# Pooled attention and a residual MLP on one core: weight sums laid out by halves, VectorE's order changed in three places, last stores on three queues

## The chip, the core and the metric

The kernel runs on one core of a Trainium2 chip. A core has a matrix engine, TensorE (PE in the profile; its weight loads are PEld), a vector engine (VectorE, DVE), an activation engine (ScalarE, ACT), a general engine (GpSimd, POOL) and a queue engine (SyncE, SP) that mostly issues DMAs. Each engine runs its own list of instructions in order, and waits on semaphores for the others. DMAs are issued by an engine, here SP, ACT or POOL, and are carried out by 16 DMA engines. The metric is the time of one execution in microseconds (us), the median of several runs. Times inside a profile are counted from the start of its span.

## The reference

```python
def _attn_ref(q, k, v):                      # B, H, S, D = 8, 8, 576, 64
    k_p = k.reshape(B, H, Sp, pool, D).mean(axis=3)      # pool = 8, Sp = 72
    v_p = v.reshape(B, H, Sp, pool, D).mean(axis=3)
    scores = scale * np.matmul(q, k_p.transpose(0, 1, 3, 2))
    ...                                      # softmax over the 72 pooled keys
    return np.matmul(attn, v_p)

def _moe_ref(x, alpha1, beta1, w_tok, alpha2, beta2, w_ch1, w_ch2, lam):
    a1 = alpha1 * x + beta1
    tok = np.einsum('ts,bsd->btd', w_tok, a1)
    u = x + lam * tok
    a2 = alpha2 * u + beta2
    ch = np.maximum(a2 @ w_ch1, 0.0) @ w_ch2             # 512 -> 2048 -> 512
    return u + lam * ch
```

The attention's output, with the heads put side by side to 512 columns, is the `x` of the second function. There are 8 x 576 = 4608 rows of 512.

## The kernel before, in words

The 4608 rows are cut into 36 chunks of 128 rows (two batches share a chunk, since 576 is four chunks and a half; the shared one has c = 4), and the chunks into nine blocks of four. Block n does the channel MLP of its four chunks; beside it, in the same stretch of time, the attention and the token mixing of batch n + 1 are computed for later blocks.

Blocks 0 and 1 do the MLP plainly. From block 2 on, the second layer (2048 to 512) is a two by two block product that is done with seven products in place of eight. The products are `L1` to `L7` (function `product`, matmuls on line L1047), and need sums of hidden values (`hidden_sum`, L1016) and sums of weights. VectorE adds the products to the residual in `gather` (steps `g1` to `g7`, L1065; in the last block the single parts of `g3` and `g5`, L1062). In blocks 7 and 8 the first layer (512 to 2048) is done with seven products as well (`hidden_product`, steps `p{q}{i}` with quarter q and product i, L1121). It needs sums of inputs (`sum_inputs`, steps `N0` to `N3`, L1104) and of first-layer weights (`sum_weights`, steps `Sb1` to `Sb4` for the front half of the columns and `Sa1` to `Sa4` for the second, L1094). Each product pair is copied out of or added to by VectorE or ScalarE (`c..`, L1134, and `d..`, L1140), and ScalarE or GpSimd write the hidden values (`r..`, L1150 for GpSimd).

Attention of batch b: SP turns the pooled k by a transposing DMA (`turn_k`, tile `kT`), VectorE finishes the pooling (`pool_k`, L645 and L651, once for each half u of the heads), TensorE computes scores (`att_S4`, L740 and L747), ScalarE the exponential, TensorE the product with v (`att_AV`, L784), and VectorE divides (L791, L793). VectorE also pools v by three additions for each half (`att_V`, L692). Token mixing is L873 on TensorE with the addition of the residual on VectorE (`mix_T`, L880), and the result is transposed by a DMA (`mix_uT`, tile `u_fm`).

Three things set the order. In blocks 0 to 6 each step carries a due time, a number in units of the block's own matmul groups; the steps are sorted by it and issued in that order. Blocks 7 and 8 follow an order written out by hand, the two strings in `late_order`. And waits are made by the tile framework: where two instructions touch overlapping regions of a tile, the later one waits for the earlier. Stores go through `store` (L970 for a plain chunk; L974 for a chunk shared by two batches, which takes two DMAs): in the last block `a0 a1 b0 b1 c0 c1 e0 e1`, where `a` and `e` are halves of the chunks 0 and 1, `b` and `c` halves of the chunks 2 and 3. Chunk 3 of the last block is a shared one.

Behind the last block GpSimd loads a flag, which `good_sums` computed from the softmax sums long before, and branches: if the flag says that the fast softmax, which leaves out the maximum, was out of its safe range, a slow exact version of all the work runs on GpSimd.

```python
again = nc.gpsimd.value_load(flag, min_val=0, max_val=1)    # L1420
with tc.If(again != 0):                                     # L1423
    exact(tc, spare, q, k, v, ...)
```

After that, the program's closing drains and semaphore events are on the last line of the kernel, L1451.

Of the kernel before, what the change touches and what calls it, by code (L numbers as in the profile page):

```python
# [9 lines left out]
BF = mybir.dt.bfloat16  # L10
# [4 lines left out]
P = 128  # L15
SPG = 72
DM = 512
# [193 lines left out]
def kernel(  # L211
# [18 lines left out]
    nc = tc.nc  # L230
# [5 lines left out]
    work = fast.enter_context(tc.tile_pool(name="work", bufs=1))  # L236
# [728 lines left out]
    def store(n, m, c0=0, c1=DM, queues=(nc.sync, nc.sync)):  # L965

        b, c = chunks[4 * n + m]
        u = u_of[n][:, m, c0:c1]
        if c < 4:
            queues[0].dma_start(  # L970
                out=out[b, 0:512, :].rearrange("(p c) d -> p c d", c=4)[:, c, c0:c1], in_=u)
        else:
            for i in range(2):
                queues[i].dma_start(out=out[b + i, 512:576, c0:c1], in_=u[64 * i:64 * i + 64, :])  # L974
# [94 lines left out]
    sums = {}  # L1069
    halves = {"C11": (0, 0), "C12": (0, 1), "C21": (1, 0), "C22": (1, 1)}  # L1070

    def weights_of(i, kc, j):

        if i < 3:
            return w1_of(kc + 2 * (i == 2), j)
        if i == 4:
            return w1_of(kc + 2, j + 8)
        t = sums["W", (1, 2, 3, 4)[(5, 6, 7, 3).index(i)]]
        c0 = 512 * (j // 4)
        return t[:, kc, c0:c0 + 512].rearrange("p (m i) -> p i m", i=4)[:, j % 4, :]  # L1080

    def sum_weights(i, g):

        if ("W", 1) not in sums:
            for k in range(2):
                t = work.tile([P, 2, 2, 1024], BF, tag="v_u", bufs=2, name="w1_s")
                sums["W", 1 + 2 * k], sums["W", 2 + 2 * k] = t[:, 0], t[:, 1]
        cols = slice(512 * g, 512 * g + 512)
        W = {k: sums["W", k][:, :, cols] for k in range(1, 5)}
        lo, hi = w1[0][:, :, cols], w1[1 + g]  # L1090
        a, b, op = {1: (hi[:, 0:2], hi[:, 2:4], ALU.add), 2: (W[1], lo[:, 0:2], ALU.subtract),
                    3: (lo[:, 0:2], hi[:, 0:2], ALU.subtract),
                    4: (lo[:, 2:4], W[2], ALU.subtract)}[i]
        nc.vector.tensor_tensor(out=W[i], in0=a, in1=b, op=op)  # L1094

# [59 lines left out]
    def block_plan(n, other):  # L1155

        plan = {"gd": good_sums}
        for q in range(4):
            for i in range(1, 8):
                plan[f"p{q}{i}"] = lambda q=q, i=i: hidden_product(n, q, i)  # L1160
            for i in range(1, 4):
                c = f"c{q}{i}"
                plan[c] = lambda q=q, i=i, c=c: hidden_copy(n, q, i, c in other)
                plan[f"d{q}{i}"] = lambda q=q, i=i: hidden_add(n, q, i)
            for k, key in (("X", "C11"), ("B", "C12"), ("Y", "C21"), ("Z", "C22")):
                for a in range(2):
                    r = f"r{q}{k}{a}"
                    plan[r] = lambda q=q, key=key, a=a, r=r: hidden_out(n, q, key, a, r in other)
        for k in range(2):
            for a in range(2):  # L1170
                t = mlp_A(n, 6 + 8 * k + a)
                plan[f"h3{'lh'[k]}{a}"] = plan[f"r3{'lh'[k]}{a}"] = lambda t=t: next(t, None)
        for g in range(2):
            for i in range(1, 5):
                plan[f"S{'ba'[g]}{i}"] = lambda i=i, g=g: sum_weights(i, g)
                plan[f"s{i}{g}"] = lambda i=i, g=g: hidden_sum(n, i, g)
        for i in range(1, 8):
            for pp in range(2):
                plan[f"L{i}{pp}"] = lambda i=i, pp=pp: product(n, i, pp)
                plan[f"g{i}{pp}"] = lambda i=i, pp=pp: gather(n, i, pps=(pp,))  # L1180
            plan[f"g{i}"] = lambda i=i: gather(n, i)
        for part in range(2):
            plan["g7" + "ab"[part]] = lambda part=part: gather(n, 7, part)
        for i in range(4):
            plan[f"N{i}"] = lambda i=i: sum_inputs(n + 1, 1 + i)
            plan[f"w{i}"] = lambda m=i: store(n, m)
        for m in range(2):
            both = (nc.sync, nc.scalar)
            plan[f"a{m}"] = lambda m=m: store(n, m, 0, HALF)
            plan[f"b{m}"] = lambda m=m: store(n, 2 + m, HALF, DM, both)  # L1190
            plan[f"c{m}"] = lambda m=m: store(n, 2 + m, 0, HALF, both)
            plan[f"e{m}"] = lambda m=m: store(n, m, HALF, DM, (both[m],) * 2)
        return plan

# [61 lines left out]
    def attention(b):  # L1256


        first = b == 1
        todo = []  # L1260
        if first:
            for hp in range(4):
                todo.append((2.6 + 0.9 * hp, lambda hp=hp: whole(att_F(b, hp))))
            todo.append((3.5, lambda: cast_rem(b, nc.gpsimd, behind=nc.vector)))
            for u in range(2):
                todo.append((3.65 + 0.1 * u, lambda u=u: load_w2(2 + u)))
            todo.append((7.4, lambda: whole(att_Frem(b, nc.scalar.copy))))
        if b < B - 1:
            at = 28.5 if first else 10.0
            todo.append((at, lambda: whole(att_F(b + 1, 0))))  # L1270
            todo.append((at + 0.1, lambda: whole(att_F(b + 1, 2))))
            todo.append((19.3 if first else 23.1, lambda: cast_rem(
                b + 1, nc.gpsimd, behind=None if first else nc.vector)))
            todo.append((26.72 if b > 1 else 27.2, lambda: whole(att_Frem(b + 1))))
        for u in range(2):
            if first:
                todo.append((3.6 + 0.1 * u, lambda u=u: sum_k(b, u, nc.gpsimd)))
            if 1 < b < B - 1:
                todo.append((26.5 + 0.1 * u, lambda u=u: sum_k(b + 1, u, nc.gpsimd)))
                todo.append((26.73 + 0.1 * u, lambda u=u: turn_k(b + 1, u)))  # L1280
            if b > 2:
                todo.append((4.1 + 2.0 * u, lambda u=u: pool_k(b, u)))
                continue
            if first:
                todo.append((19.1 + 0.1 * u, lambda u=u: sum_k(2, u, nc.gpsimd)))
            todo.append((7.0 + 2.3 * u if first else 2.9 + 2.0 * u,
                         lambda u=u: whole(
                             att_K(b, u, nc.vector.tensor_copy if first else nc.scalar.copy))))
        for u in range(2):
            at = (9.0 if first else 6.3, 13.6)[u]  # L1290
            todo.append((at, lambda u=u: att_S4(b, u)))
            for k, dt in enumerate((0.1, 0.1, 0.1, 0.7, 1.7, 1.75) if u else (0.1, 0.1, 0.1, 1.1, 2.1, 3.1)):
                todo.append((at + dt, lambda u=u, k=k: st1[b]["exp", u](k)))
            early = (5.2, 5.7, 3.7, 4.2) if first else (5.7, 6.2, 2.9, 3.4)
            for i, dt in enumerate((2.9, 3.4, 4.6, 5.1) if u else early):
                h = 4 * u + i
                todo.append((at + dt, lambda h=h: whole(att_AV(b, h))))
                if i % 2:
                    eng = nc.gpsimd if h == 5 or first and h < 5 else nc.vector
                    todo.append((at + dt + 0.1, lambda h=h, eng=eng: att_X(b, h - 1, h + 1, eng)))  # L1300
        for u in range(2):
            when = (0.2, 1.4, 2.2), (10.0, 12.8, 13.0) if b == 2 else (5.0, 7.2, 8.0)
            if first:
                when = (10.6, 10.7, 10.8), (12.5, 12.6, 12.7)
            for i, at in enumerate(when[u]):
                todo.append((at, lambda u=u, i=i: att_V(b, u, 4 >> i)))
        for c in range(5):
            at = 22.0 + 1.1 * c if first else 21.0 + (1.3 if b == 2 else 1.15) * c
            if c < 4 or b % 2:
                todo.append((at, lambda c=c: whole(mix_T(b, c))))  # L1310
                key = (b, c) if c < 4 else (b - 1, 4)
                todo.append((at + 1.8, lambda key=key: whole(mix_uT(key))))
        return todo
# [11 lines left out]
        SUMS + 1: (  # L1325
# [10 lines left out]
    for n in range(NBLK):  # L1336
# [54 lines left out]
                todo.append((27.2 if m < 2 else 29.2, lambda m=m: store(n, m)))  # L1391
        if n == SUMS - 1:
            for i in range(1, 5):
                todo.append((27.3 + 0.01 * i, lambda i=i: sum_inputs(n + 1, i)))
        if n == 0:
            todo.append((6.2, lambda: whole(setup_rowsum(4))))
            todo.append((10.0, lambda: load_lam(nc.vector)))
# [58 lines left out]
```

## Time and profile before

| | |
|---|---|
| median of 3 runs | 328.36 us (328.30 to 328.98) |
| the profiled execution | 328.99 us, span 327.5 us |
| TensorE busy | 318.5 us, 97% of the span, 2556 matmuls |
| VectorE busy | 259.5 us, 79% |
| ScalarE busy | 180.3 us, 55% |
| GpSimd busy | 133.1 us, 41% |

A row of a timeline gives the start and the length in us, the engine and line, the operation with the tile written and the tiles read, and in brackets the idle time of the engine ahead of it with the instruction that ended it; rows with xN hold N instructions in a row. The lengths of TensorE's matmuls are modelled and overlap, so that the step from one start to the next is what counts. Rows of an engine's name with a q (POOLq, SPq) belong to its instruction queue: loads of registers, branches, events, drains and DMA issues, which are not counted as busy.

### The profile page before, as it was taken

To read this page: it belongs to the slowest core of one execution; us is meant where nothing else is said; L and a number is where in the kernel's file an instruction comes from. 1 tells how busy PE (TensorE), PEld (TensorE's weight loads), DVE (VectorE), ACT (ScalarE), POOL (GpSimd) and SP (SyncE) were. 2 spreads that over 40 slices of the span, in tenths; PEclk is the share of its full clock that TensorE was granted. 3 is DMA by queue.
4 is the path that set the end of the run, shared out by engine and by line. 5 is a ranking of instruction groups with operands and counts; after the bars stand their busy time and mean duration, and the time that the engine had idled before them with its cause. 6 is when DMAs were issued, how large, how long until landed. Compare 5 with 4: busy or idle time off the path is not lost.

```text
span 327.5 us, 6744 instructions
## 1 busy us (share of the span) xinstructions
PE 318.5 (97%) x2556; PEld 214.8 (66%) x2556; DVE 259.5 (79%) x538; ACT 180.3 (55%) x353; POOL 133.1 (41%) x155
## 2 busy tenths in 40 slices
PE   8899999999999999999999999999999999999994
PEld 3689654455444576657675676567755766988983
DVE  6783578987599979786967796878697889888984
ACT  3868999278224843396139612881278136823920
POOL 8587467994274022601180018002600650711900
PEclk9999999999999999999999999999999999999999
DMA  7999999868997971698549944997470034003003
GB/s 198 203 230 255 213 175 284 141 191 158 193 214 117 219 211 35 102 280 154 155 76 268 172 137 87 164 222 204 90 163 0 2 65 146 0 2 109 23 20 112
DMA packets 73352, 47.43 MB, mean 145 GB/s; under 512 B 41282, under 2 KB 64098, under 8 KB 73318
## 3 DMA queue, kind: packets, MB, share of 16 engines
q1 hardware_dynamic: 59302, 34.78, 45.2%
q0 software_dynamic: 12896, 11.28, 22.3%
q10 hardware_dynamic: 1120, 0.92, 0.9%
q8 instruction: 20, 0.33, 0.4%
q14 instruction: 14, 0.11, 0.1%
HBM read 38.31 MB, written 9.44 MB: 146 GB/s over the span
## 4 chain that ended last, share of the span: by engine, by line
PE 81%; DVE 5%; DMA 5%; POOL 3%; issue 3%; ACT 2%; POOLq 0%; SPq 0%; DVEq 0%; ACTq 0%
PE ps_h L930 27%; PE ps_w L1047 23%; PE ps_tok L873 11%; PE ps_ch L951 8%; PE ps_m L1121 5%; DMA v<-in_v_dram 2%; DMA kT<-k_bf 2%; PE ps_av L784 2%; PE ps_s L740 2%; POOL k_bf L362 1%; ACT H L938 1%; DVE x_tm L793 1%; POOL k_raw L360 1%; DVE u_sb L1065 1%; DVE w_s L1094 1%
## 5 line engine op out<-in xcount | busy, mean ns | idle before, releaser
L930 PE MATMUL ps_h<-u_fm,w 128*128 128x512 bf16 (+2 forms) x496 | 108.8, 366 | 0.6 <-ACT u_fm L905 0.4
L938 ACT ACTIVATE H<-ps_h,bias_cols 128x512 bf16<-128x512 f32 x116 | 79.0, 688 | 37.7 <-PE ps_h L930 36.4
L930 PEld LDWEIGHTS <-w 128*128 128x128 bf16 x496 | 53.0, 114 | 39.6 <-issue 2.1
L1047 PEld LDWEIGHTS <-H 128*128 128x128 bf16 x560 | 53.4, 98 | 10.4 <-DVE u_sb L1065 1.2
L884 ACT CAST u_bf<-u_sb 128x512 bf16<-128x512 f32 x34 | 21.0, 618 | 70.0 <-issue 41.5
L807 POOL TENSOR_TENSOR xs<-x_tm,lamal_bc 128x512 bf16<-128x512 f32 x12 | 15.2, 1270 | 103.8 <-DVE x_tm L793 103.5
L1047 PE MATMUL ps_w<-w,H 128*128 128x256 bf16 x448 | 53.6, 273 | 0.0
L1065 DVE TENSOR_TENSOR u_sb<-u_sb,ps_w 128x512 f32<-128x512 f32 x54 | 36.1, 684 | 12.0 <-PE ps_w L1047 11.5
L873 PE MATMUL ps_tok<-xs,wtT 128*128 128x512 bf16 (+5 forms) x220 | 45.1, 361 | 0.0
L793 DVE TENSOR_TENSOR x_tm<-ps_av,recs 128x320 f32<-128x320 f32 x64 | 31.5, 492 | 2.7
L880 DVE TENSOR_TENSOR u_sb<-x_tm,ps_tok 128x512 f32<-128x512 f32 (+1 forms) x40 | 27.2, 683 | 7.5 <-PE ps_tok L873 7.3
L769 ACT ACTIVATE ET<-ps_s 72x512 f16<-72x512 f32 x56 | 32.3, 590 | 0.0
L951 PE MATMUL ps_ch<-w,H 128*128 128x512 bf16 x128 | 30.4, 379 | 0.0
L873 PEld LDWEIGHTS <-wtT 128*128 128x128 bf16 (+3 forms) x220 | 19.2, 100 | 15.2 <-issue 1.1
L791 DVE RECIPROCAL recs<-ps_av 128x5 f32<-128x5 f32 x64 | 12.1, 188 | 17.4 <-PE ps_av L788 17.1
L692 DVE TENSOR_TENSOR v_u<-v_u 72x1024 f32<-72x1024 f32 (+1 forms) x24 | 23.9, 995 | 0.2
L1047 PE MATMUL ps_w<-w_t,h_s 128*128 128x256 bf16 x168 | 22.6, 272 | 0.0
L951 PEld LDWEIGHTS <-H 128*128 128x128 bf16 x128 | 12.0, 98 | 13.9 <-issue 0.4
L360 POOL TENSOR_TENSOR k_raw<-k_raw 128x512 f32<-128x512 f32 x14 | 19.1, 1366 | 2.2 <-DMA k_raw<-in_k_dram 2.2
L362 POOL TENSOR_TENSOR k_bf<-k_raw 128x512 bf16<-128x512 f32 x14 | 19.1, 1364 | 1.1
L1047 PEld LDWEIGHTS <-h_s 128*128 128x128 bf16 x168 | 16.4, 98 | 4.2
L784 PEld LDWEIGHTS <-ET 72*128 72x128 f16 x256 | 13.8, 97 | 5.6 <-ACT ET L726 0.2
(188 smaller groups left out, 470.6 us busy)
## 6 DMA issues: line engine op xcount, KB each, us to landing
out_dram<-u_sb SPq DMA_DIRECT2D x29, 256.0 KB, 3.9
k_raw<-in_k_dram SPq DMA_DIRECT2D x13, 512.0 KB, 4.4
v_u<-in_v_dram SPq DMA_DIRECT2D x12, 512.0 KB, 6.1
q_bf<-in_q_dram POOLq DMA_DIRECT2D x15, 256.0 KB, 5.1
w<-in_moe_w_ch_dram POOLq DMA_DIRECT2D x6, 512.0 KB, 13.2
out_dram<-u_sb SPq DMA_DIRECT2D x11, 128.0 KB, 2.8
v<-in_v_dram POOLq DMA_DIRECT2D x4, 288.0 KB, 10.6
w<-in_moe_w_ch_dram POOLq DMA_DIRECT2D x1, 1024.0 KB, 14.0
```

Of the source, the lines that this page charges most:

```text
L360: eng.tensor_tensor(out=raw[:, :, 0:2], in0=raw[:, :, 0:2], in1=raw[:, :, 2:4], op=ALU.add)
L362: eng.tensor_tensor(out=bf, in0=twice[0], in1=twice[1], op=ALU.add)
L692: nc.vector.tensor_tensor(out=out, in0=source[:, :, 0:width], in1=source[:, :, width:2 * width], op=ALU.add)
L769: nc.scalar.activation(out=o, in_=i, func=AF.Exp, bias=0.0, scale=0.125 if b < 3 else 0.125 * 0.125)
L793: nc.vector.tensor_tensor(out=x[:, 1 - odd:6 - odd, dd:dd + D], in0=av[:, :, 0:64], in1=rec.unsqueeze(2).to_broadcast((P, 5, D)), op=ALU.mult)
L873: nc.tensor.matmul(out=ps_tok[p0:p1, cols], lhsT=wtT[0:kk, at, P * c:P * c + p1 - p0], rhs=xs_pool[i][0:kk, sc, cols], start=(sc == 0), st ...
L880: nc.vector.tensor_tensor(out=s["u"][p0:p1, :], in0=x[p0:p1, 1 + c if c < 4 else 5 - 5 * i, :], in1=ps_tok[p0:p1, 0:DM], op=ALU.add)
L930: nc.tensor.matmul(out=ps_h[:, t0:t1 + one], lhsT=w1_of(cc, j), rhs=rhs, start=(cc == 0), stop=(cc == 3))
L938: nc.scalar.activation(out=H4[n, j // 4][:, j % 4, :], in_=ps_h, func=AF.Relu, bias=bias_cols[:, j:j + 1], scale=1.0)
L951: nc.tensor.matmul(out=ps, lhsT=H_of(n, j)[:, 128 * m:128 * m + 128], rhs=w2[j // 4][:, j % 4, :], start=(j == 0), stop=(j == NJ - 1))
L1047: nc.tensor.matmul(out=ps, lhsT=stat(j), rhs=moving(j), stop=(j == 7), start=(first and (pp == 0 or alone) and j == 0), skip_group_check=True)
L1065: nc.vector.tensor_tensor(out=o, in0=o, in1=banks[key, "both"], op=ALU.add)
```

## The change

Five edits, each of which leaves the arithmetic as it is:

1. The four sums of first-layer weights, each 128 x 2 x 1024 before with the two halves as column ranges, are laid out as two contiguous blocks of 128 x 1024, one for each half.
2. In block 6 the input sums for block 7 have earlier due times: 25.3 and 25.31 for the first two, 26.0 and 26.01 for the others, where all four had 27.3.
3. In block 7 the gather `g3` and the stores of chunks 0 and 1 stand ahead of the last product's second half (`L71`) and of its gathers and stores.
4. The second half's `pool_k` has due time 8.95 in place of 6.1, which puts it behind two value sums and two hidden sums on VectorE in five blocks.
5. The stores `b` and `c` of the last block are spread over SP, ACT and POOL. Before, SP issued b0, b1's first part, c0, c1's first part and e0, and ACT issued b1's and c1's second parts and e1. After, SP issues b0, c1's second part and e0, ACT issues b1's and c1's first parts and e1, and POOL issues b1's second part and c0, both ahead of the flag's load. `b1`'s parts wait for gather `g7b`, and `c0` for gather `g4`.

TensorE's and ScalarE's order of instructions is the same in both kernels.

```diff
 def weights_of(i, kc, j):
-        c0 = 512 * (j // 4)
-        return t[:, kc, c0:c0 + 512].rearrange("p (m i) -> p i m", i=4)[:, j % 4, :]
+        return t[:, j // 4, kc, :].rearrange("p (m i) -> p i m", i=4)[:, j % 4, :]
 def sum_weights(i, g):
-                t = work.tile([P, 2, 2, 1024], BF, tag="v_u", bufs=2, name="w1_s")
+                t = work.tile([P, 2, 2, 2, 512], BF, tag="v_u", bufs=2, name="w1_s")
-        W = {k: sums["W", k][:, :, cols] for k in range(1, 5)}
+        W = {k: sums["W", k][:, g] for k in range(1, 5)}
 def block_plan(n, other):
-            both = (nc.sync, nc.scalar)
+            both, third = (nc.sync, nc.scalar), nc.gpsimd
+            q_b, q_c = ((nc.sync,), (nc.scalar, third))[m], ((third,), (nc.scalar, nc.sync))[m]
-            plan[f"b{m}"] = lambda m=m: store(n, 2 + m, HALF, DM, both)
-            plan[f"c{m}"] = lambda m=m: store(n, 2 + m, 0, HALF, both)
+            plan[f"b{m}"] = lambda m=m, to=q_b: store(n, 2 + m, HALF, DM, to)
+            plan[f"c{m}"] = lambda m=m, to=q_c: store(n, 2 + m, 0, HALF, to)
 def attention(b):
-                todo.append((4.1 + 2.0 * u, lambda u=u: pool_k(b, u)))
+                todo.append(((4.1, 8.95)[u], lambda u=u: pool_k(b, u)))
 late_order, block 7:
-            "... N0 N2 N1 L30 N3 L31 L70 L71 g7a g7b w2 w3 g3 w0 w1",
+            "... N0 N2 N1 L30 N3 L31 L70 g3 w0 w1 L71 g7a g7b w2 w3",
 block 6:
-                todo.append((27.3 + 0.01 * i, lambda i=i: sum_inputs(n + 1, i)))
+                todo.append(((25.3, 25.31, 26.0, 26.01)[i - 1], lambda i=i: sum_inputs(n + 1, i)))
```

2 rows, old and new, of the table late_order are left out of this document.

## The prediction

> **What bounds the kernel now.** I read the page first, for the busy shares and the chain, then PE's waits in the late blocks, then timelines around each wait, and last the issue rows after the last matmul. All times are us from the start of the span.
>
> ```profile
> span 327.5 us, 6744 instructions
> PE 318.5 (97%) x2556; PEld 214.8 (66%) x2556; DVE 259.5 (79%) x538; ACT 180.3 (55%) x353; POOL 133.1 (41%) x155
> PE 81%; DVE 5%; DMA 5%; POOL 3%; issue 3%; ACT 2%; POOLq 0%; SPq 0%; DVEq 0%; ACTq 0%
> ```
>
> TensorE (PE) carries 81% of the chain and is busy 97% of the span. The change adds and removes no matmul, so it can win only where PE waits and after PE's last matmul. From 268 on, PE's waits are these two groups:
>
> ```profile
> PE ps_m L1121 <- DVE w_s L1094: 1.0, 2, 0.7
> PE ps_m L1121 <- DVE h_q L1134: 0.4, 1, 0.4
> ```
>
> The profiled execution took 328.99, 1.49 more than its span and 0.63 more than the median of the runs, 328.36.
>
> **Part 1: weight sums half by half (L1072 to L1094).** Before, the two halves of a sum are column ranges of one tile, interleaved in memory. PE around the waits:
>
> ```profile
> 276.24 0.27 PE L1121 MATMUL ps_m<-u_s,w_s 128*128 128x256 bf16 x1
> 276.75 0.52 PE L1121 MATMUL ps_m<-u_s,w_s 128*128 128x256 bf16 x3 [0.24 <-DVE w_s L1094]
> 277.11 0.60 PE L1121 MATMUL ps_m<-u_fm,w 128*128 128x256 bf16 x4
> 277.54 0.27 PE L1121 MATMUL ps_m<-u_s,w_s 128*128 128x256 bf16 x1
> 278.55 0.52 PE L1121 MATMUL ps_m<-u_s,w_s 128*128 128x256 bf16 x3 [0.74 <-DVE w_s L1094]
> ```
>
> and VectorE (DVE) beside them:
>
> ```profile
> 274.99 0.68 DVE L1094 TENSOR_TENSOR w_s<-w,w 128x1024 bf16<-128x1024 bf16 x1
> 276.00 0.69 DVE L1094 TENSOR_TENSOR w_s<-w_s,w 128x1024 bf16<-128x1024 bf16 x1 [0.33 <-PE ps_m L1121]
> ...
> 277.81 0.69 DVE L1094 TENSOR_TENSOR w_s<-w,w 128x1024 bf16<-128x1024 bf16 x1
> ```
>
> By the written order of block 7 (front half Sb, second half Sa) the held products are p06 and p17, which read half 0 of sums 2 and 3. Half 0 of sum 3 is the row at 274.99, done at 275.67, and sum 2 stands before it. But the waits end with the other half: Sa2 at 276.00 + 0.69 = 276.69 and Sa3 at 277.81 + 0.69 = 278.50. PE is held for sums that it does not read, and Sa2 itself waited 0.33 for PE in the same way. Four unbroken matmuls take 277.54 − 277.11 = 0.43, or 0.11 each. So the stretch 276.24 to 276.75 lost 0.51 − 0.11 = 0.40, and 277.54 to 278.55 lost 1.01 − 0.11 = 0.90. With each half contiguous those dependences are gone, and the sums that PE does read were done at least 0.6 before it asks. **−1.3.** What would be late next are ACT and POOL (55% and 41% busy), which write the hidden values after PE; I take nothing from them. The sums keep size and type, so 0.69 should hold.
>
> **Part 2: input sums earlier, in block 6.** Four L1104 instructions of 0.42 move ahead on DVE, the first two past the last token-mix addition, which starts after an idle 0.52:
>
> ```profile
> 268.07 1.38 DVE L880 TENSOR_TENSOR u_sb<-x_tm,ps_tok 64x512 f32<-64x512 f32 x2 [0.52 <-PE ps_tok L873]
> ...
> 270.52 0.42 DVE L1104 TENSOR_TENSOR u_s<-u_fm 128x512 bf16<-128x512 bf16 x1
> ```
>
> PE has no wait on any of them. Two take 2 × 0.42 = 0.84, less the idle 0.52: at most +0.3 for the last chunk's transpose, whose reader has other products ahead of it; and the weight sums behind may start up to 0.3 earlier, which after part 1 nobody waits for. **0**, ends −0.3 and +0.3.
>
> **Part 3: g3 and stores w0, w1 ahead of the last product, block 7.** PE, then DVE:
>
> ```profile
> 297.74 2.35 PE L1121 MATMUL ps_m<-u_fm,w 128*128 128x256 bf16 x20
> 300.48 1.03 PE L1121 MATMUL ps_m<-u_s,w_s 128*128 128x256 bf16 x8 [0.39 <-DVE h_q L1134]
> ```
> ```profile
> 297.94 1.88 DVE L1065 TENSOR_TENSOR u_sb<-u_sb,ps_w 128x512 f32<-128x512 f32 x3 [0.69 <-PE ps_w L1047]
> 299.75 0.68 DVE L1134 COPY h_q<-ps_m 128x512 f32<-128x512 f32 x1
> ```
>
> At 297.94 DVE starts three gathers together, because g7a and g7b wait for the last product and g3 stands behind them; the copy for which PE waits starts at 299.75. With g3 ahead, one of three (1.88 / 3 = 0.63) moves into the 0.69 that DVE idles, so the copy starts about 0.6 earlier and PE's wait ends. Twenty matmuls at 0.11 last issue at 297.74 + 19 × 0.11 = 299.83, the next would be at 299.94: the loss is 300.48 − 299.94 = **−0.53**. SP issues w0 and w1 earlier and w2, w3 later, with nothing behind them for 20 us.
>
> **Part 4: second pooled-k addition later, in five blocks.**
>
> ```profile
>   DMA kT<-k_bf: 4.0, 3
> ```
> ```profile
> 176.78 0.42 DVE L645 TENSOR_TENSOR kp<-kT 128x256 bf16<-128x256 bf16 x1 [2.02 <-DMA kT<-k_bf]
> 178.98 0.69 DVE L1016 TENSOR_TENSOR h_s<-H 128x1024 bf16<-128x1024 bf16 x1
> ```
> ```profile
> 182.76 0.30 PE L740 MATMUL ps_s<-qT,kp 64*72 64x256 bf16 x1 [0.20 <-DVE x_tm L793]
> ...
> 182.97 0.28 PE L740 MATMUL ps_s<-qT,kp 64*72 64x256 bf16 x1
> 183.38 1.49 PE L930 MATMUL ps_h<-u_fm,w 128*128 128x512 bf16 x6
> ```
>
> Three of these additions (L645) hold DVE 4.0 in all for a transposing DMA; of the blocks concerned PE feels it in this one. There two value sums and two hidden sums now go first. They end at 178.98 + 0.69 = 179.67 today, up to 2.02 earlier without the wait, so the addition ends between 178.1 and 180.1, and the scores that read it, which PE works on at 182.76, keep over 2 us. PE's loss there is at most 0.20 shown plus the hole 182.97 to 183.38 less a step of 0.11, 0.3, so **0 to −0.5**. Whether the DMA is that late in the median run isn't known. It could be what separates 328.99 from 328.36; then it is worth −0.5 against the profiled run, and 0 against the median.
>
> **Part 5: last stores on three queues.** The same eight DMAs; SP loses b1's first part and c0, ACT swaps its two parts for two others, POOL takes b1's second part and c0. Today, SP's first and last issue of five, ACT's last, the landing view of these stores, and DVE's last additions:
>
> ```profile
> 321.96 0.33 SPq L970 DMA_DIRECT2D out_dram<-u_sb  x1
> ...
> 324.06 0.54 SPq L970 DMA_DIRECT2D out_dram<-u_sb  x1
> ```
> ```profile
> 323.72 0.37 ACTq L970 DMA_DIRECT2D out_dram<-u_sb  x1
> ```
> ```profile
> DMA to landing us min/median/max: 2.5/2.5/2.5
> ```
> ```profile
> 320.64 1.88 DVE L1065 TENSOR_TENSOR u_sb<-u_sb,ps_w 128x512 f32<-128x512 f32 x3 [0.46 <-PE ps_w L1047]
> 322.44 0.41 DVE L1062 TENSOR_TENSOR u_sb<-u_sb,ps_w 128x256 f32<-128x256 f32 x1
> 323.26 0.42 DVE L1062 TENSOR_TENSOR u_sb<-u_sb,ps_w 128x256 f32<-128x256 f32 x1 [0.40 <-PE ps_w L1047]
> ```
>
> The last landing is 324.06 + 2.5 = 326.56. With SP relieved, e0 goes out near 323.1, after its addition (322.44 + 0.41 = 322.85), and the last to land is e1, issued by ACT at 323.72 as now: 326.2. For the transfers alone: −0.35, at best −0.9 (e0's whole advance).
>
> ```profile
> 323.00:324.50 1.50, 0.23 (x3) 0.00 (x0) 0.42 (x1) 0.00 (x0) 0.00 (x0) 1.00 0.88 237
> ```
>
> The DMA engines are 88% busy just after the last matmul, so more queues share them. The Trainium skill, page "DMA: Bandwidth & Descriptors", section "Issuing engines are not separate DMA queues", says that transfers issued by different engines run on the same 16 engines and that only the issuing time is saved; by that the gain is the 0.35 and not the 0.9.
>
> **What POOL has behind its stores.** POOL ends the program: it loads a flag and branches over the slow version of the kernel. Rows by line:
>
> ```profile
> L1420 POOLq TENSOR_LOAD <-flag x1: 502/502/502, 310.3 to 310.3; - x1
> ```
> ```profile
> L1423 POOLq EVENT_SEMAPHORE  x2: 17/17/17, 313.8 to 313.9; - x2
> L1423 POOLq COMPARE_BRANCH  x1: 50/50/50, 311.2 to 311.2; - x1
> ```
> ```profile
> L1451 POOLq EVENT_SEMAPHORE  x4: 17/17/17, 326.7 to 327.4; - x4
> L1451 POOLq DRAIN  x3: 46/102/2770, 314.0 to 327.2; - x3
> ```
>
> Load at 310.3; branch at 311.2; then nothing until 313.8 (2.6 gone behind a taken branch); then a drain at 314.0. The 2.77 drain must be this first one, as the others stand at the closing events from 326.7 on. So the path takes 314.0 + 2.77 − 310.3 = 6.5 and ends at 316.8, hidden today, since the stores keep everyone until 326.7. That cover goes. After the change POOL's queue holds b1's second part and c0 first, and c0 waits for g4, the end of DVE's three gathers, 320.64 + 1.88 = 322.5. How long POOL takes to issue one is seen early in the kernel:
>
> ```profile
> L371 POOL DMA_DIRECT2D wt_bf<-in_moe_w_tok_dram x2: 573/581/589, 6.5 to 7.1; - x2
> ```
>
> So the load starts between 322.5 (no issue time) and 323.1 (0.58), and POOL is ready for the closing events between 329.0 and 329.6, or 329.9 if the branch's fetch runs 0.3 longer among the stores. Against 326.7 that is +2.3 to +3.2; I take c0's issue as shown, 323.1, and +2.8, since fetch and drain have a row each. The landing gain vanishes under it. The Trainium skill, page "Runtime: NRT & Kernel Launch", section "Instruction fetch mechanics", speaks against this edit too: a taken branch to outside the loaded window waits for a DMA fetch of the target. The 2.6 row agrees.
>
> **Sum.** Profiled run: 328.99 − 1.3 − 0.53 − 0.5 + 2.8 = 329.5. From the median: 328.36 − 1.3 − 0.53 + 2.8 = 329.3 if the late DMA was not in it, 328.8 if it was. I take **329.2**, the likeliest case's own range being 328.5 to 330.0.
>
> **The rivals.** Differences under 0.2%, 0.66, count as none: 327.7 to 329.0.
>
> Other side, faster: the drain is short. The other two POOL drains took 0.05 and 0.10, and what the 2.77 does isn't shown; if it belongs to the moment (a fetch that the stalled queue has since done), the path is 6.5 − 2.7 = 3.8, ready at 326.3 to 326.9, −0.4 to +0.2 against now, and the time is 328.36 − 1.83 − 0.4 … + 0.2 = 326.1 to 326.7. It turns at a path of 6.5 − (2.8 − 1.83) = 5.5: a drain under 1.8 makes the kernel faster. Against it: the one execution shown has the row, and the branch target is the same. The Trainium skill, page "VectorE: DVE Perf Modes", section "The DRAIN you can't avoid", gives closing drains as about 12 ns on all engines; by it the time is as in this case, but the 2770 ns row disagrees.
>
> Slower still: parts 1 and 3 give nothing, because the wait only changes its name (DVE at 79% hands PE the next sum late, or POOL's hidden values come late): 328.36 + 2.8 = 331.2, or 330.2 with half the gain. For it: DVE is busy 79% of the span, and more than that among those sums. Against: the half that the held products read was done 0.6 and more before.
>
> Doing nothing: the late DMA of part 4 does not recur and part 2 is hidden; that is inside the main case's range.
>
> **How the numbers follow.** Path pays in full 0.61: three quarters of it above 329.0, the rest within 0.2%. Short drain 0.26, all faster. Gains lost 0.13, nearly all slower. Faster 0.27, same 0.17, slower 0.56. The range, 326.2 to 330.2, holds the short drain, the main case and the nearer end of the lost gains, because the drain has ends on both sides.
>
> **What would show it.** Right: no L1121 wait on L1094 or on L1134 at g3; POOL's load after 321 instead of 310, a gap of 2.6 behind its branch, a drain of 2.8, and closing events some 2 behind the last landing. Wrong: a short drain, closing events straight after the landing, or new PE waits in the last two blocks.

## The result and the profile after

The changed kernel takes 330.53 us (median of 5 runs, 330.12 to 330.71); the kernel before took 328.37 beside it. It is slower by a ratio of 1.006, 95% interval 1.0045 to 1.0075. The forecast said 329.2, with 326.2 to 330.2 as its range: the direction was right, the size too small, +0.8 where +2.2 came, and the time lies above the range.

PE did win what it was to win. This is the view of all its waits over the whole span of the changed kernel (us in all, times, longest):

```profile
PE ps_warm L862 <- DVE early L402: 1.5, 1, 1.5
PE ps_v L680 <- DMA v<-in_v_dram: 0.4, 1, 0.4
PE ps_sc L702 <- ACT kp L671: 0.4, 1, 0.4
PE ps_h L930 <- ACT u_fm L905: 0.4, 1, 0.4
PE ps_bc L496 <- DVE part L476: 0.2, 1, 0.2
PE ps_w L516 <- DMA wt_bf<-in_moe_w_tok_dram: 0.2, 1, 0.2
```

No L1121 wait is left (the line is L1120 now); the rest are from the start of the kernel. The tail undoes it. First DVE's last additions in the changed kernel's timeline, then POOL's rows by line. In the latter the counts are followed by the shortest, median and longest duration in ns and by the first and the last start.

```profile
318.42 1.88 DVE L1065 TENSOR_TENSOR u_sb<-u_sb,ps_w 128x512 f32<-128x512 f32 x3 [0.47 <-PE ps_w L1047]
320.22 0.41 DVE L1062 TENSOR_TENSOR u_sb<-u_sb,ps_w 128x256 f32<-128x256 f32 x1
321.04 0.42 DVE L1062 TENSOR_TENSOR u_sb<-u_sb,ps_w 128x256 f32<-128x256 f32 x1 [0.41 <-PE ps_w L1047]
```
```profile
320.00 0.58 POOL L974 DMA_DIRECT2D out_dram<-u_sb  x1 [10.71 <-DVE u_sb L1065]
320.60 0.58 POOL L970 DMA_DIRECT2D out_dram<-u_sb  x1
```
```profile
L1420 POOLq TENSOR_LOAD <-flag x1: 688/688/688, 320.6 to 320.6; - x1
```
```profile
L1423 POOLq EVENT_SEMAPHORE  x2: 17/17/17, 325.1 to 325.2; - x2
L1423 POOLq COMPARE_BRANCH  x1: 45/45/45, 321.6 to 321.6; - x1
```
```profile
L1451 SPq EVENT_SEMAPHORE  x12: 17/28/1109, 321.5 to 328.9; - x12
L1451 POOLq EVENT_SEMAPHORE  x4: 17/17/17, 328.2 to 328.9; - x4
L1451 POOLq DRAIN  x3: 46/103/2933, 325.2 to 328.7; - x3
L1451 SPq DRAIN  x3: 7/7/13, 325.4 to 328.4; - x3
```

DVE ends its last addition at 321.46 (321.04 + 0.42); before, that was at 323.68, so the computing ends 2.2 earlier. POOL's closing events begin at 328.2, 6.7 later; before, it was 326.7 − 323.68 = 3.0. The tail grew by 3.7. POOL loads the flag at 320.6, branches at 321.6, goes on at 325.1 and drains for 2.93. SP waits for the landings and for POOL's event at 325.1, and has its first drain at 325.4, so every store has landed 2.8 or more before POOL's closing events.

Some executions of the later comparisons ran at a lower granted clock (0.97 to 0.98) and took at least 3.6 us longer; the medians and ranges below leave them out, the ratios of the late flag and of the earlier input sums still hold some of them, and the late flag's profile is one of them.

### The profile page after: what moved, and what is told of

The parts are those of the page before. It is cut to its first block, busy times and chain, and to the rows that moved or that the text cites. A ratio compares the mean times of both kernels' runs of the same rounds, so it can differ in the third digit from the quotient of the medians.

```text
span 329.0 us, 6714 instructions
## 1 busy us (share of the span) xinstructions
PE 316.2 (96%) x2528; PEld 214.8 (65%) x2556; DVE 259.4 (79%) x538; ACT 179.9 (55%) x353; POOL 134.6 (41%) x157
## 4 chain that ended last, share of the span: by engine, by line
PE 89%; DMA 3%; POOL 2%; ACT 2%; DVE 1%; issue 1%; POOLq 0%; DVEq 0%; ACTq 0%
PE ps_h L930 30%; PE ps_w L1047 26%; PE ps_tok L873 12%; PE ps_ch L951 8%; PE ps_m L1120 6%; DMA wt_bf<-in_moe_w_tok_dram 3%; PE ps_s L740 2%; PE ps_av L784 2%; ACT H L938 1%; PE ps_r L747 1%; POOL v L308 1%; PE ps_av L788 1%; ACT ET L769 0%; DVE h_xs L1133 0%; ACT u_fm L905 0%
## 5 line engine op out<-in xcount | busy, mean ns | idle before, releaser
L930 PE MATMUL ps_h<-u_fm,w 128*128 128x512 bf16 (+2 forms) x478 | 107.2, 366 | 1.2 <-ACT u_fm L905 0.4
```

The costliest lines, as they stand in the source:

```text
L930: nc.tensor.matmul(out=ps_h[:, t0:t1 + one], lhsT=w1_of(cc, j), rhs=rhs, start=(cc == 0), stop=(cc == 3))
```

## The experiments

**The changed kernel with the old stores.** Edits 1 to 4 stay, edit 5 goes.

```diff
-            both, third = (nc.sync, nc.scalar), nc.gpsimd
-            q_b, q_c = ((nc.sync,), (nc.scalar, third))[m], ((third,), (nc.scalar, nc.sync))[m]
+            both = (nc.sync, nc.scalar)
...
-            plan[f"b{m}"] = lambda m=m, to=q_b: store(n, 2 + m, HALF, DM, to)
-            plan[f"c{m}"] = lambda m=m, to=q_c: store(n, 2 + m, 0, HALF, to)
+            plan[f"b{m}"] = lambda m=m: store(n, 2 + m, HALF, DM, both)
+            plan[f"c{m}"] = lambda m=m: store(n, 2 + m, 0, HALF, both)
```

> The changed kernel with its last stores on SP and ACT alone, as before. Theory 1 (POOL's end path, from the flag's load to the closing drain, ends last because stores stand ahead of it): the path is hidden again, PE's gains stay: 328.4 - 1.3 - 0.5 = 326.5, or 326.0 if the late kT transfer also counts. Theory 2 (the moved sums and additions cost time somewhere, and the tail only shows it): 328.4 or more.

Measured: 326.42 (326.25 to 326.54) beside 328.50 of the kernel before, ratio 0.9934, 0.9921 to 0.9947. POOL's rows of the closing line are those of before again:

```profile
L1450 POOLq EVENT_SEMAPHORE  x4: 17/17/17, 324.3 to 324.9; - x4
L1450 POOLq DRAIN  x3: 46/103/2770, 311.5 to 324.8; - x3
L1450 SPq DRAIN  x3: 7/7/13, 324.2 to 324.5; - x3
```

The long drain starts at 311.5 and is over ten us before the closing events (311.5 + 2.77 = 314.3, against 324.3), and the closing events follow SP's first drain, 324.2. So the loss is in edit 5 alone; edits 1 to 4 are worth 2.1.

**The kernel before with three queues.** Edit 5 alone, as in the diff of the change.

> The kernel before with the last stores on three queues and nothing else. Theory 1: the tail grows by what the profile after shows, from 3.5 to 7.15 between the end of the last matmul and POOL's closing events, +3.6: 332.0. The forecast's own sizes (2.6 behind the branch, 2.8 of drain) give +2.8: 331.2. Theory 2: about 328.4, the tail costing nothing by itself.

Measured: 332.16 (331.90 to 332.43; ratio 1.0109, 1.0093 to 1.0125), 3.7 above the 328.50 of the kernel before beside it. By itself the edit costs as much as the profile after says. Taking it away from the changed kernel gained 4.1. The profiles lie between: 3.7 in the tail, and some 0.2 outside the span, since the changed kernel's profiled execution took 1.71 more than its span (330.71 − 329.0), against 1.49 before and 1.54 with the old stores. That makes 3.9; the 0.2 to either side are not accounted for.

**The flag's load ahead of the stores.** The branch stays behind them.

```diff
+                if n > SUMS and name == "b0":
+                    again = nc.gpsimd.value_load(flag, min_val=0, max_val=1)
                 todo[name]()
...
-    again = nc.gpsimd.value_load(flag, min_val=0, max_val=1)
```

> The changed kernel with POOL's load of the flag ahead of its two stores, the branch still behind them. If the path is a plain chain (load, branch, fetch, drain), the load's 1.0 drops out: 329.5. If the fetch behind the branch waits until the stores' transfers are through (it started when they ended), an earlier branch only waits longer: 330.3 to 330.5.

Measured: 329.16 (328.79 to 329.46), 1.4 below the changed kernel: more than the plain chain's 1.0, and the rival's 330.3 is out. POOL's rows at the branch and the close:

```profile
L1424 POOLq EVENT_SEMAPHORE  x2: 17/17/17, 323.8 to 323.9; - x2
L1424 POOLq COMPARE_BRANCH  x1: 50/50/50, 320.5 to 320.5; - x1
```
```profile
L1452 POOLq EVENT_SEMAPHORE  x4: 17/17/17, 327.0 to 327.6; - x4
L1452 POOLq DRAIN  x3: 46/103/2933, 324.0 to 327.5; - x3
```

The branch is 1.1 earlier (320.5, not 321.6), goes on 3.3 later, and the same drain follows; the closing events are 1.2 earlier (327.0, not 328.2). What stands ahead of the branch moves the end about one for one.

**A near target for the branch.** The slow version is replaced by one memset.

```diff
     with tc.If(again != 0):
-        exact(tc, spare, q, k, v, ...)
+        nc.gpsimd.memset(spare.tile([1, 8], FP, name="spare"), 0.0)
```

> The changed kernel with the slow version behind the branch replaced by one memset, so that the branch's target is near (the fallback for unsafe softmax sums is left out). If gap and drain are code fetches behind a far jump: the gap of 3.45 and the drain of 2.9 go, POOL is ready before the last store lands, and the time is 326.0, as low as without POOL's stores or 0.3 lower. If they belong to the branch or to POOL's drain behind its own DMAs: 330.5, with the drain still at 2.8 or more.

Measured: 326.74 (326.66 to 327.24), ratio 0.9945, 0.9932 to 0.9958: 0.3 above the old stores, where 0 to 0.3 below was expected. The rows at the branch and the close:

```profile
L1423 POOLq COMPARE_BRANCH  x1: 54/54/54, 321.5 to 321.5; - x1
L1423 POOLq EVENT_SEMAPHORE  x1: 17/17/17, 321.7 to 321.7; - x1
```
```profile
L1450 POOLq EVENT_SEMAPHORE  x4: 17/17/17, 324.8 to 325.4; - x4
L1450 POOLq DRAIN  x3: 46/101/2933, 321.8 to 325.2; - x3
L1450 SPq DRAIN  x3: 7/7/13, 324.2 to 325.0; - x3
```

This parts the two terms, which the expectation had taken together. The gap behind the branch falls from about 3.4 (3.5 by starts that are rounded to 0.1, 3.4 by the sum of the path further down) to 0.2: it belonged to the far target. The Trainium skill, page "Runtime: NRT & Kernel Launch", section "Instruction fetch mechanics", says that a taken branch to outside the loaded window has to wait until a DMA has fetched the target, and this pair of rows agrees. The drain stays at 2.93, with no far target and no fetch beside it, so it is not a code fetch; what it does is open. POOL's closing events, at 324.8, still come 0.6 behind SP's first drain, so with this drain behind its stores POOL is the last to end even here. The same rows price edit 5's transfers. SP's first drain, after its last landing, is at 324.2 here with three queues and at 324.2 with two. DVE's last addition ended at 321.33 (320.91 + 0.42) here and at 321.24 (320.82 + 0.42) there, so three queues landed the stores 0.1 sooner, not 0.35:

```profile
320.91 0.42 DVE L1062 TENSOR_TENSOR u_sb<-u_sb,ps_w 128x256 f32<-128x256 f32 x1 [0.41 <-PE ps_w L1047]
```
```profile
320.82 0.42 DVE L1062 TENSOR_TENSOR u_sb<-u_sb,ps_w 128x256 f32<-128x256 f32 x1 [0.40 <-PE ps_w L1047]
```

**A late flag without stores on POOL.** The old stores, and POOL copies one element of chunk 2 behind `c0` ahead of the flag's load.

```diff
... (the stores as in the first experiment; spot is a new tile of one element)
                 todo[name]()
+                if n > SUMS and name == "c0":
+                    nc.gpsimd.tensor_copy(out=spot, in_=u_of[n][0:1, 2, 0:1])
```

> The changed kernel with its last stores on SP and ACT alone, and on POOL one copy of a single element of chunk 2 behind gather g4, ahead of the flag's load: POOL's end path starts as late as with the stores, but POOL issues no DMA. If the longer path (the fetch came 1.8 behind the branch where it was 0.94, the drain took 2.93 where it was 2.77) is owed to the stores' traffic on the DMA engines: the same lengths, 330.3 to 330.5. If it is owed to POOL's own two DMA issues: 0.94 and 2.77 again, 329.2 to 329.5.

Measured: 329.82 (329.54 to 330.30), 1.6 above the 328.19 of the kernel before beside it (ratio 1.0022, 0.998 to 1.006), between the two expectations. The rows split the question. POOL's rows at the branch and the close, of which only the steps from one to the next are read:

```profile
L1425 POOLq EVENT_SEMAPHORE  x2: 17/17/17, 329.9 to 330.0; - x2
L1425 POOLq COMPARE_BRANCH  x1: 50/50/50, 326.6 to 326.6; - x1
```
```profile
L1453 POOLq DRAIN  x3: 46/103/2770, 330.1 to 333.4; - x3
```

The long drain is 2.77 again: its extra 0.16 goes with POOL's own DMAs. The gap stays long, 3.3. To see why, the DMA view of a window shows the instruction queue, q14, and the stores' queues (packets, MB, share of the 16 engines). The kernel before, 312.1 to 312.7:

```profile
q14 instruction: 1, 0.01, 4.4%
```

the changed kernel, first 321.6 to 323.4 and then 323.4 to 323.9:

```profile
q10 hardware_dynamic: 185, 0.17, 37.6%
q1 hardware_dynamic: 212, 0.18, 35.1%
q0 software_dynamic: 49, 0.13, 21.0%
```
```profile
q14 instruction: 1, 0.01, 3.9%
```

and the late flag, 328.2 to 328.7:

```profile
q10 hardware_dynamic: 96, 0.09, 50.7%
q1 hardware_dynamic: 72, 0.06, 43.4%
q14 instruction: 1, 0.01, 3.8%
```

Before, the fetch's packet came 0.9 to 1.5 after the branch (311.2), on idle DMA engines. In the changed kernel nothing of q14 moves until 1.8 after the branch, while the stores hold 94% of the engines; with the late flag it is 1.6 or more, with no store on POOL. From the start of the packet's window to POOL's next row it is 1.7 in all three (312.1 to 313.8, 323.4 to 325.1, 328.2 to 329.9), so the longer gap is all ahead of the packet. So the fetch is held up by the stores' transfers, whoever issues them, though not until they are all through: in the last window it moves among them. How they hold it up is not shown.

**The other edits one by one, on the kernel before.** Each is the edit's own part of the change's diff.

> The kernel before with the weight sums laid out half by half and nothing else. Theory 1 (the waits were for the other half's sum): both L1094 waits gone, 328.4 - 1.3 = 327.1. Rival (the waits only take another name): 328.4, with a new PE wait in the same place.

Measured for the weight sums by halves: 327.01 (326.80 to 327.43), ratio 0.9956, 0.9938 to 0.9973: −1.3 against 328.32. PE's waits from 268 on in that kernel:

```profile
PE ps_m L1120 <- DVE h_q L1133: 0.4, 1, 0.4
```

Both waits for the sums are gone and none took their place; the rival falls.

> The kernel before with g3 and its stores ahead of L71 and nothing else. Theory 1: the wait for the copy of h_q gone, 328.4 - 0.5 = 327.9. Rival (the gathers g7a and g7b, now later, hold the next products): 328.4 or more.

Measured for g3 ahead of L71: 327.76 (327.57 to 328.66), ratio 0.998, 0.9967 to 0.9994: −0.6. From 268 on PE waits only for the weight sums:

```profile
PE ps_m L1121 <- DVE w_s L1094: 1.0, 2, 0.7
```

> The kernel before with the second pooled-k addition later and nothing else. If the kT transfer is late in every execution: 328.4 - 0.5 = 327.9 and its spread falls. If it is late only in the executions near 329.0: about 328.3, the high ones gone. Theory 2 (the addition now comes late for the scores): above 328.4 with a PE wait of L740 or L747 on kp.

Measured for the later pooled-k addition: 328.28 (328.08 to 328.60) beside 328.32 (327.90 to 329.80), ratio 0.9998, 0.9987 to 1.0009. The median does not move. Five of the 23 runs of the kernel before stood above 328.6, none of these nine; chance alone would do that about once in nine times, so the runs don't show that the high ones are gone. The traces say what a high execution is. Here are DVE's first and second pooled-k addition in the block of part 4 and the first of the next block, in the kernel before (profiled at 328.99; its second one is in the prediction, with a wait of 2.02), then in the weight sums by halves (327.43, the highest of its runs), then in the kernel before with three queues:

```profile
172.01 0.41 DVE L645 TENSOR_TENSOR kp<-kT 128x256 bf16<-128x256 bf16 x1
...
207.32 0.41 DVE L645 TENSOR_TENSOR kp<-kT 128x256 bf16<-128x256 bf16 x1
```
```profile
172.17 0.41 DVE L645 TENSOR_TENSOR kp<-kT 128x256 bf16<-128x256 bf16 x1
...
176.68 0.42 DVE L645 TENSOR_TENSOR kp<-kT 128x256 bf16<-128x256 bf16 x1 [1.77 <-DMA kT<-k_bf]
...
207.23 0.42 DVE L645 TENSOR_TENSOR kp<-kT 128x256 bf16<-128x256 bf16 x1
```
```profile
171.98 0.41 DVE L645 TENSOR_TENSOR kp<-kT 128x256 bf16<-128x256 bf16 x1
...
175.12 0.42 DVE L645 TENSOR_TENSOR kp<-kT 128x256 bf16<-128x256 bf16 x1 [0.39 <-DMA kT<-k_bf]
...
206.56 0.41 DVE L645 TENSOR_TENSOR kp<-kT 128x256 bf16<-128x256 bf16 x1
```

From the first row to the last it is 35.31, 35.06 and 34.58: 0.7 and 0.5 more where DVE waited 2.02 and 1.77 for the kT transfer than where it waited 0.39, which is about what these two executions stand above their medians (0.6 and 0.4). PE's list of waits shows 0.20 of it in the one and nothing in the other, so that list alone would have missed it.

> The kernel before with block 6's input sums earlier and nothing else. Theory 1: 328.4, hidden. Bounds of the forecast: -0.3 to +0.3.

Measured for the earlier input sums: 328.11 over five runs, beside 328.19 over fifteen of the kernel before (ratio 1.0012, 0.996 to 1.0063). Hidden, within 0.1.

**A better split of the stores over two queues.** Edits 1 to 4, and c1's first part on ACT rather than SP.

```diff
             both = (nc.sync, nc.scalar)
+            q_c = ((nc.sync,), (nc.scalar, nc.scalar))[m]
...
-            plan[f"c{m}"] = lambda m=m: store(n, 2 + m, 0, HALF, both)
+            plan[f"c{m}"] = lambda m=m, to=q_c: store(n, 2 + m, 0, HALF, to)
```

> The changed kernel with its last stores on SP and ACT alone, and c1's first part moved from SP to ACT (SP: b0, b1's first part, c0, e0; ACT: b1's second part, both parts of c1, e1). If the last landing is set by SP's fifth issue, e0 lands 0.5 earlier and the time is up to 0.4 below the same kernel with the old stores (326.4): 326.0 to 326.2. If it is set by what the 16 DMA engines can move, 326.4.

Measured: 326.30 (326.20 to 326.47) beside 328.32, ratio 0.9934, 0.9919 to 0.9949; with the old stores it was 0.9934 as well. SP's fifth issue was not the limit. Either version is the fastest seen, 2.0 to 2.1 below the kernel before.

## Why the prediction came out as it did

Right, with its size: **part 1** forecast −1.3, measured −1.3; **part 3** −0.53 (its own rows give 0.54), measured −0.6; **part 2** 0, measured −0.1 with that much noise. The one by one gains add to 2.0, and the kernel with all of them gained 2.1. The rival by which these waits only change their names fell with the two single edits, where no new wait came up.

**Part 4** left open whether the late kT transfer was in the median; it was not. So the sum was the upper of its two, 329.3, and not the 329.2 that was taken between 328.8 and 329.3. The profile that was read was one of the high executions, and there the late transfer cost 0.7, not the 0.5 at most.

**Part 5** holds the step that failed, and it failed by its size. The mechanism, POOL's load, branch and drain behind its stores, was right: without the stores on POOL the loss is gone, with them alone it is there. But "+2.8" (the forecast's own 323.1 + 6.5 − 326.7 gives 2.9), with +3.2 as its far end, measured 3.7 alone, and 4.1 taken away from the changed kernel. The failed step is the length of POOL's path in its new place: it was taken over as the path that "takes 6.5", and the changed kernel's took 328.2 − 320.6 = 7.6. Of the 1.1 more, the load has 0.19 (688 ns for 502) and the drain 0.16; the other 0.8 is the gap behind the branch, 2.6 before and so about 3.4 now, because the fetch came later among the stores. The forecast had allowed 0.3 for this, "if the branch's fetch runs 0.3 longer among the stores", as an upper end. It had priced a path by its length on idle DMA engines, and moved it to the one stretch of the end where its own row showed them 88% busy. The start went the other way. The forecast took 323.1, the upper of its bounds 322.5 and 323.1; POOL's load started at 320.6, which is 322.8 on the clock of before (2.2 later), half way between them. There POOL had just issued b1's second part (320.00 + 0.58), the issue of c0 began beside the load, and the load did not wait for its end. So 0.3 less at the start and 1.1 more on the path make 3.7 of 2.9. The 0.2 outside the span was in no term.

The gain of the transfers, −0.35 at best −0.9, measured 0.1. The Trainium skill, page "DMA: Bandwidth & Descriptors", section "Issuing engines are not separate DMA queues", has it that only the issuing time is saved; the runs agree in kind and show 0.1, less than the 0.35 that was worked out.

The rival of a short drain is out: POOL's first closing drain was 2.77 or 2.93 in each profile shown here. The Trainium skill, page "VectorE: DVE Perf Modes", section "The DRAIN you can't avoid", gives about 12 ns for the drains ahead of and behind a program on all engines; that does not hold for POOL's first closing drain in any of these runs.

## What to carry to other kernels

Before work is put on a quiet engine near the end, read what that engine still has to do behind it, and price it under the traffic of its new place, not of its old one. A second half that is a column range of a tile can cost a wait that nobody needs: here a contiguous half of its own gained 1.3, more than any of the reorderings. And where a profiled execution stands above the median, ask first which of its waits the median doesn't have.

## What the runs showed of the hardware

POOL's first closing drain takes 2.77, or 2.93 where POOL issued DMAs shortly before, with or without a far branch ahead of it; its cause isn't known from these runs. A taken branch over the slow version took 2.6 to POOL's next row on idle DMA engines and 3.3 to 3.4 among stores, and 0.2 with a near target. The profiled executions whose POOL issued stores at the end took 1.71 to 1.76 beyond their span, the others 1.45 to 1.54; why was not tried.
